# Attention and gated MLP on one core: the last two token chunks become one of 1024 tokens, worked in two stages

## The chip, the cores and the metric

The kernel runs on one core of a Trainium2 chip. The metric is the device time of one execution in microseconds (us). A profile of one execution gives the span of the program, the work of each engine and every instruction's start and length. PE is the matrix engine (PEld its weight loads), DVE the vector engine, ACT the scalar engine, POOL the GpSimd engine, SP the engine that issues most transfers; SPq and ACTq are transfers that SP and ACT issue.

## The reference

All inputs are fp32. The attention's queries are [8, 8, 576, 64] (batch, heads, tokens, features); keys and values are averaged over groups of 8 tokens, so each query sees 72 keys. The attention's output, as 4608 tokens of 512 features, goes through a layer of 2048 hidden features.

```
k_p, v_p = mean over 8 tokens of k, v            # 72 keys a head
attn     = softmax(q @ k_p.T / sqrt(64)) @ v_p
x   = attn.transpose(0, 2, 1, 3).reshape(4608, 512)
h   = x @ w_in                                   # 512 x 2048
g   = h * sigmoid(1.702 * h)
out = g @ w_out                                  # 2048 x 512
```

## The kernel before

**Precision.** Every product is made three times on rounded operands: each operand is split into a high part (a cast) and a low part (value minus cast), and high times high, low times high and high times low are added in the same bank of PSUM. A product of a block therefore is three matmuls for each 128 features that are summed over.

**Chunks.** Of each batch the first 512 tokens are a chunk (0 to 7); the last 64 tokens of the eight batches together are chunk 8. The tokens left over go through DRAM (left) until chunk 8 gathers them. Chunks 0 and 1 use plain products. Chunks 2 to 8 make h with seven products of blocks instead of eight: `pair(c, p)` (line 2345) takes pair p of eight (256 of the 2048 hidden features) and multiplies sums of blocks of the weights (tiles ws, 1.75 MB for a pair, fetched from DRAM by `fetch_pair` for every chunk anew) with sums of blocks of the tokens (x, xs, made by `combine`). Each of the seven products is six matmuls of 256 columns (line 2370) into the banks ha or hb. The helpers around them: `keep` (line 2385) copies a bank to SBUF, by ACT or DVE; `plus` (line 2392) adds a bank to the copy, on DVE; `gelu` applies the gate twice on ACT (lines 2409 and 2417), and line 2424 subtracts for the low part, on POOL or DVE.

**Output.** `outputs` (line 2556) gives blocks of 128 tokens by 512 output features, three matmuls of 512 columns each (lines 2572 to 2574), that are put between the products of the following pair and accumulate over the eight pairs in banks o. The weights w_out (tiles w1_0 to w1_15) stay in SBUF as high and low part. `finish` (line 2115) copies each o to SBUF and stores it; in chunk 8 by DVE or ACT (lines 2131 and 2143) with two stores of 128 KB for each copy.

**Order.** A planner in the program sorts all work by due times and costs into one list, two tables shift or swap single tasks of the list, and the list's order is that of each engine's queue.

## Time and profile before

| | before |
|---|---|
| time, median of 3 runs | 895.14 us (894.18 to 896.23) |
| span of the profiled execution | 893.6 us |
| PE busy | 880.5 us (99%) |
| DVE, ACT, POOL busy | 636.7 (71%), 543.8 (61%), 307.6 us (34%) |
| read from and written to DRAM | 150.47 and 25.17 MB |

The profiled execution has no time of its own beside its span: 893.6 us from the first to the last event of the program, 1.5 us less than the median of the runs. A busy share is an average over the program; idle time of an engine costs nothing unless something that sets the end waits for it. The three rounds of runs before spread over 2.05 us.

### The profile page before, as it was taken

To read this page: it belongs to the slowest core of one execution; us is meant where nothing else is said; L and a number is where in the kernel's file an instruction comes from. 1 tells how busy PE (TensorE), PEld (TensorE's weight loads), DVE (VectorE), ACT (ScalarE), POOL (GpSimd) and SP (SyncE) were. 2 spreads that over 40 slices of the span, in tenths; PEclk is the share of its full clock that TensorE was granted. 3 is DMA by queue.
4 is the path that set the end of the run, shared out by engine and by line. 5 is a ranking of instruction groups with operands and counts; after the bars stand their busy time and mean duration, and the time that the engine had idled before them with its cause. 6 is when DMAs were issued, how large, how long until landed. Compare 5 with 4: busy or idle time off the path is not lost.

```text
span 893.6 us, 15818 instructions
## 1 busy us (share of the span) xinstructions
PE 880.5 (99%) x5452; PEld 788.0 (88%) x5452; DVE 636.7 (71%) x1272; ACT 543.8 (61%) x1232; POOL 307.6 (34%) x301
## 2 busy tenths in 40 slices
PE   7999999999999999999999999999999999999997
...
PEclk9999999999999999999999999999999999999999
...
GB/s 262 378 242 65 195 71 197 201 171 189 170 273 166 229 229 250 225 176 218 229 230 155 231 187 263 165 205 231 218 192 154 199 232 184 172 187 212 165 143 47
DMA packets 145263, 176.68 MB, mean 198 GB/s; under 512 B 85664, under 2 KB 96928, under 8 KB 145184
## 3 DMA queue, kind: packets, MB, share of 16 engines
...
HBM read 150.47 MB, written 25.17 MB: 197 GB/s over the span
## 4 chain that ended last, share of the span: by engine, by line
PE 94%; SPq 2%; ACT 2%; DMA 1%; issue 0%; POOL 0%; DVE 0%; POOLq 0%; ACTq 0%
PE ha L2370 18%; PE hb L2370 14%; PE o L2574 12%; PE o L2573 12%; PE o L2572 12%; PE sps L1656 4%; PE h L2165 3%; PE h L2167 3%; PE h L2166 3%; PE o L2208 3%; PE o L2209 3%; PE o L2207 3%; PE pav L1895 1%; PE pav L1898 1%; PE pav L1897 1%; PE pav L1896 1%
## 5 line engine op out<-in xcount | busy, mean ns | idle before, releaser
L2574 PE MATMUL o<-w,glall 128*128 128x512 f32 x448 | 176.4, 394 | 0.0
L2572 PE MATMUL o<-w,ghall 128*128 128x512 f32 x448 | 176.3, 394 | 0.0
L2573 PE MATMUL o<-w,ghall 128*128 128x512 f32 x448 | 176.1, 393 | 0.0
L2424 POOL TENSOR_TENSOR glall<-shared,ghall 128x256 fp32r<-128x256 f32 x83 | 66.3, 804 | 215.5 <-ACT shared L2417 135.7
L2574 PEld LDWEIGHTS o<-w,glall 128*128 128x128 f32 x448 | 84.3, 188 | 18.5
L2409 ACT ACTIVATE ghall<-shared 128x256 fp32r<-128x256 f32 x150 | 61.3, 415 | 63.2 <-DVE shared L2392 32.5
L2370 PEld LDWEIGHTS ha<-xs,ws 128*128 128x128 f32 x672 | 93.1, 189 | 7.2 <-ACT shared L2385 0.8
L2370 PE MATMUL ha<-xs,ws 128*128 128x256 f32 x672 | 98.9, 283 | 0.0
L2370 PE MATMUL hb<-x,ws 128*128 128x256 f32 x672 | 94.5, 284 | 0.0
L2370 PEld LDWEIGHTS hb<-x,ws 128*128 128x128 f32 x672 | 88.8, 189 | 4.0 <-DVE shared L2392 0.3
L2572 PEld LDWEIGHTS o<-w,ghall 128*128 128x128 f32 x448 | 84.7, 189 | 8.5
L2573 PEld LDWEIGHTS o<-w,ghall 128*128 128x128 f32 x448 | 84.1, 188 | 8.6
L2392 DVE TENSOR_TENSOR shared<-shared,hb 128x256 f32<-128x256 f32 x112 | 46.6, 417 | 59.1 <-PE hb L2370 49.2
L2385 ACT COPY shared<-ha 128x256 f32<-128x256 f32 x93 | 34.4, 370 | 64.1 <-PE ha L2370 63.3
L2424 POOL TENSOR_TENSOR glall<-gall,ghall 128x256 fp32r<-128x256 f32 x46 | 35.6, 776 | 109.3 <-ACT gall L2417 75.5
L2165 PE MATMUL h<-x,w 128*128 128x256 f32 (+1 forms) x192 | 63.3, 329 | 1.5 <-ACT gh L2187 1.0
L2417 ACT ACTIVATE shared<-shared 128x256 f32<-128x256 f32 x150 | 60.8, 415 | 5.1 <-ACT osb L2125 1.3
L2167 PE MATMUL h<-x,w 128*128 128x256 f32 (+1 forms) x192 | 61.2, 319 | 0.0
L2166 PE MATMUL h<-x,w 128*128 128x256 f32 (+1 forms) x192 | 61.2, 319 | 0.0
L2424 DVE TENSOR_TENSOR glall<-shared,ghall 128x256 fp32r<-128x256 f32 x67 | 34.0, 509 | 38.1 <-ACT shared L2417 29.4
L2195 POOL TENSOR_TENSOR gl<-g,gh 128x512 fp32r<-128x512 f32 x28 | 39.5, 1410 | 48.9 <-ACT gh L2187 35.6
L1771 ACT COPY main<-sc 32x256 f32<-32x256 f32 (+2 forms) x109 | 48.7, 447 | 2.9 <-DVE sc L1728 1.1
(189 smaller groups left out, 2049.2 us busy)
## 6 DMA issues: line engine op xcount, KB each, us to landing
...
```

Of the source, the lines that this page charges most:

```text
L1771: copy(out=main()[32 * r : 32 * (r + 1), :, cols].rearrange("p j t (k a) -> p t j a k", a=2), in_=sc()[rows, ts, :, 16 * r : 16 * (r + 1)] ...
L2165: nc.tensor.matmul(o, lhsT=w[:, 0, j], rhs=xs[:, 0], start=j == 0, stop=False)
L2166: nc.tensor.matmul(o, lhsT=w[:, 1, j], rhs=xs[:, 0], start=False, stop=False)
L2167: nc.tensor.matmul(o, lhsT=w[:, 0, j], rhs=xs[:, 1], start=False, stop=j == NJ - 1)
L2370: nc.tensor.matmul(o, lhsT=wv()[:, r, jj], rhs=xo(k, jj), start=start and n == 0, stop=n == len(terms) - 1,  skip_group_check=not start,)
L2392: lambda: nc.vector.tensor_tensor(out=part(i), in0=part(i), in1=hb()[:, half * 256 : half * 256 + 256], op=ALU.add),
L2409: lambda: nc.scalar.activation(out=gh(), in_=src(), func=AF.Gelu_apprx_sigmoid),
L2417: lambda: nc.scalar.activation(out=part(i), in_=src(), func=AF.Gelu_apprx_sigmoid),
L2424: engine.tensor_tensor(out=gl(), in0=part(i), in1=gh().bitcast(F32), op=ALU.subtract)
L2572: nc.tensor.matmul(o(), lhsT=gh()[:, tok], rhs=w()[:, 0], start=start, stop=False)
L2573: nc.tensor.matmul(o(), lhsT=gh()[:, tok], rhs=w()[:, 1], start=False, stop=False)
L2574: nc.tensor.matmul(o(), lhsT=gl()[:, tok], rhs=w()[:, 0], start=False, stop=stop)
```

## The change

Chunks 7 and 8 are now one chunk (`LATE = 7`) of 1024 tokens, two halves of 512: batch 7's first 512 tokens and the 512 left tokens, all of which are gathered ahead of it (`gather_left`). Its operands (`late_op`, tiles y11, y21, y22, yt1 to yt4, each of 512 columns for two blocks) are made by `late_combine` and `late_split`; y22_1 takes the place of xs6_3, an operand that the last product hb6_7 of chunk 6 reads. The chunk runs in two stages, called stage B and stage C here.

Stage B, `hidden(p)` for all eight pairs in turn: seven products of six matmuls of 512 columns (new line 2154) into the banks la, lb and lc (a pair's lb takes the bank of the pair before); keep, plus and gelu are on 512 columns, and the gated h stays in SBUF (tiles store). Beside it `fold_out(p)` makes sums of the blocks of w_out on POOL and DVE and writes them to DRAM (768 KB for each pair).

Stage C, `outgoing(th, p)` for the two halves th of the tokens and the eight pairs: the sums of w_out come back (`fetch_sums`), `operands` makes sums and splits of the stored g (new lines 2325 and 2331), and seven products of six matmuls of 256 columns (new line 2376) accumulate over the eight pairs in seven banks m1 to m7. `combined(th)` then makes the four blocks of the output of seven banks, by one copy and seven additions on DVE (new line 2409), and stores 512 KB after each two blocks.

```diff
-    for c in range(FROM, B + 1):
+    for c in range(FROM, LATE):
...
+    def hidden(p):
...
+        product("11", "11", ha, True)
+        keep(at(0, 0), ha)
+        product("12", "21", hb, True)
+        plus(at(0, 0), hb)
+        gelu(at(0, 0))
+        product("s2", "t2", ha, False)
+        keep(at(0, 1), ha)
+        product("s1", "t1", hc, True)
+        product("s3", "t3", ha, False)
+        keep(at(1, 1), ha)
+        plus(at(1, 1), hc)
+        gelu(at(1, 1))
+        product("22", "t4", ha, False)
+        keep(at(1, 0), ha)
+        gelu(at(1, 0))
+        product("s4", "22", hc, False)
+        plus(at(0, 1), hc)
+        gelu(at(0, 1))
...
+    def late_combine(piece):
+
+        late_split("22", piece, "t2")
+        for out, a, b in (("t1", "t3", "t1"), ("t3", "t2", "t3"), ("t2", "t2", "t1"), ("t4", "t4", "t2")):
+            out, a, b = (x_whole(f"l{piece}", n) for n in (out, a, b))
+            less(out, a, b, a.refs() + b.refs(), out.refs())
+        for n in ("t1", "t3", "t2", "t4"):
+            late_split(n, piece, n)
...
+    def fold_out(p):
...
+            either(512, sums, [f], [(u, 2 * i), (u, 2 * i + 1)])
+        for out, a, b in ((0, 1, 0), (1, 3, 1), (3, 3, 0), (2, 3, 2)):
...
+            either(256, less_of, [(u, a), (u, b)], [(u, out)])
...
+    def operands(th, p):
...
+        parts_of(512, lambda: g()[:, :, 0:256], [g], a[0], a[1], ref(a[0]), ref(a[1]))
+        parts_of(256, at(1, 1), [g], lambda: a22()[:, 0], lambda: a22()[:, 1], (a22, 0), (a22, 1))
...
+        sums(views[1], at(1, 0), at(1, 1), ALU.add, [g], keys[1])
+        sums(views[3], at(0, 0), at(1, 0), ALU.subtract, [g], keys[3])
+        sums(views[2], views[1], at(0, 0), ALU.subtract, [g, keys[1]], keys[2])
+        sums(views[4], at(0, 1), views[2], ALU.subtract, [g, keys[2]], keys[4])
+        for s, u, names in ((s13, u13, (1, 3)), (s24, u24, (2, 4))):
+            parts_of(512, u, [keys[i] for i in names], s[0], s[1], ref(s[0]), ref(s[1]))
...
+    def outgoing(th, p):
...
+        a, t = operands(th, p), folded[p]
+        for m in "1675432" if p == NPAIR - 1 else "1245763":
...
+    def combined(th):
...
+        copy(512, lambda copy: copy(out=cells(a1), in_=bank("1")()), [bank("1")], [ref(a1)])
...
+        add(u2, a1, "6")
+        add(u3, u2, "7")
+        add(at(1, 1), u3, "5")
+        add(u2, u2, "5")
+        add(at(1, 0), u3, "4", ALU.subtract)
+        store_rows(th, 1, osbs[1])
+        add(at(0, 1), u2, "3")
+        add(at(0, 0), a1, "2")
+        store_rows(th, 0, osbs[0])
```

`either` and `sums` issue on POOL or, with the star below, on DVE; `parts_of` is a cast (ACT or DVE) and a subtraction by `either`. The planner and its tables are gone too: the order of all tasks is written out in a string `ORDER`, with a letter for the kind of work (P for PE, V for DVE, G for POOL, A for ACT, D for a transfer) and a star where a task goes to the other of its two engines, as in `*A:ah0_0#2 A:at0_0#0 A:at0_1#0`. PE's order is the same as before, row for row, up to the last matmul before chunk 7.

The first place is PE's start of chunk 7. Here ha7_0 and hb6_7 are banks of `pair`, o6 the output blocks of chunk 6, la, lb and lc the banks of `hidden`, and the x3 or x6 at a row's end counts matmuls. Before:

```order
L2370 MATMUL ha7_0_8582<-x7_8115,ws7_0_0_8372 128x256 x6
L2572 MATMUL o6_256_7700<-w1_12_1333,ghall1_2994 128x512
L2573 MATMUL o6_256_7700<-w1_12_1333,ghall1_2994 128x512
L2574 MATMUL o6_256_7700<-w1_12_1333,glall1_3077 128x512
L2572 MATMUL o6_384_7729<-w1_12_1333,ghall1_2994 128x512
L2573 MATMUL o6_384_7729<-w1_12_1333,ghall1_2994 128x512
L2574 MATMUL o6_384_7729<-w1_12_1333,glall1_3077 128x512
L2572 MATMUL o6_0_7629<-w1_14_1513,ghall0_2943 128x512
L2573 MATMUL o6_0_7629<-w1_14_1513,ghall0_2943 128x512
L2574 MATMUL o6_0_7629<-w1_14_1513,glall0_2961 128x512
L2370 MATMUL hb6_7_8502<-xs6_3_7411,ws6_7_2_8343 128x256 x6
```

Now, at the same place:

```order
L2154 MATMUL la0_8620<-y11_0_8144,ws7_0_0_8397 128x512 x3
L2154 MATMUL la0_8620<-y11_1_8166,ws7_0_0_8397 128x512 x3
L2086 MATMUL o6_256_7716<-w1_12_1349,ghall1_3010 128x512
L2087 MATMUL o6_256_7716<-w1_12_1349,ghall1_3010 128x512
L2088 MATMUL o6_256_7716<-w1_12_1349,glall1_3093 128x512
L2154 MATMUL lb0_8635<-y21_0_8187,ws7_0_0_8397 128x512 x3
L2154 MATMUL lb0_8635<-y21_1_8233,ws7_0_0_8397 128x512 x3
L2086 MATMUL o6_384_7746<-w1_12_1349,ghall1_3010 128x512
```

And 29 rows further, where the last output block of chunk 6 has been issued:

```order
L2154 MATMUL la0_8620<-yt2_0_8688,ws7_0_2_8509 128x512 x3
L2154 MATMUL la0_8620<-yt2_1_8690,ws7_0_2_8509 128x512 x3
L2154 MATMUL lb1_8753<-y21_0_8187,ws7_1_0_8546 128x512 x3
L2154 MATMUL lb1_8753<-y21_1_8233,ws7_1_0_8546 128x512 x3
```

Products of 512 columns in three banks stand where products of 256 columns stood; the output blocks of chunk 6 are between them as before, and after the last of those PE's queue holds products of `hidden` alone.

The second place is DVE's queue from the last product hb6_7 of chunk 6 on. L2392 before is `plus`; now L1904 is `plus` of `pair`, L1523 a low part of an operand, L1459 a sum of operands, L2221 a sum of w_out's blocks, L2171 `plus` of `hidden`. Before:

```order
L2392 TENSOR_TENSOR shared12_2909<-shared12_2909,hb6_7_8502 128x256
L2385 COPY gall_3045<-ha7_0_8582 128x256
L2392 TENSOR_TENSOR gall_3045<-gall_3045,hb7_0_8631 128x256
L2385 COPY shared12_2909<-ha7_0_8582 128x256
L2392 TENSOR_TENSOR shared12_2909<-shared12_2909,hb7_0_8631 128x256
L2424 TENSOR_TENSOR glall0_2961<-gall_3045,ghall0_2943 128x256
L2392 TENSOR_TENSOR gall_3045<-gall_3045,hb7_0_8631 128x256
```

Now, the rows from the fourth to the fifteenth row behind hb6_7's addition (the two rows of two inputs ahead of them are the low part of y22_1, 256 columns, and a sum of operands, 512 columns):

```order
L1516 CAST yt2_1_8690<-xtl1_1_7908 128x256
L1459 TENSOR_TENSOR xtl1_0_8452<-xtl1_0_8452,xtl1_1_7908 128x512
L1516 CAST yt2_1_8690<-xtl0_2_7958 128x256
L1523 TENSOR_TENSOR yt2_0_8688<-xtl1_1_7908,yt2_0_8688 128x256
L1523 TENSOR_TENSOR yt2_1_8690<-xtl0_2_7958,yt2_1_8690 128x256
L1523 TENSOR_TENSOR yt2_1_8690<-xtl1_1_7908,yt2_1_8690 128x256
L1516 CAST yt4_1_8707<-xtl0_0_8113 128x256
L1523 TENSOR_TENSOR yt4_0_8700<-xtl1_0_8452,yt4_0_8700 128x256
L1523 TENSOR_TENSOR yt4_1_8707<-xtl0_0_8113,yt4_1_8707 128x256
L1523 TENSOR_TENSOR yt4_1_8707<-xtl1_0_8452,yt4_1_8707 128x256
L2221 TENSOR_TENSOR u0_8730<-w1_1_483 128x512
L2171 TENSOR_TENSOR store0_0_8724<-store0_0_8724,lb0_8635 128x512
```

What DVE did for pair 0 of chunk 7 after hb6_7 (copies and additions of banks) has become the rest of the merged chunk's operands, and the addition that empties the bank lb0 stands behind all of them. POOL's queue holds, in the same stretch, five two-operand instructions of 256 columns (y22_1, yt2, the low part gl of pair 7 of chunk 6, yt4, one sum of u0) and three of 512 (two sums of operands and one of w_out's blocks).

The third place is the end of the program. PE before, the last two output blocks:

```order
L2572 MATMUL o8_384_9574<-w1_15_1577,ghall1_2994 128x512
L2573 MATMUL o8_384_9574<-w1_15_1577,ghall1_2994 128x512
L2574 MATMUL o8_384_9574<-w1_15_1577,glall1_3077 128x512
L2572 MATMUL o8_384_9574<-w1_14_1513,ghall1_2994 128x512
L2573 MATMUL o8_384_9574<-w1_14_1513,ghall1_2994 128x512
L2574 MATMUL o8_384_9574<-w1_14_1513,glall1_3077 128x512
```

PE now, the last pair of the second half, and DVE's last seven instructions (128x2x256 is the same 512 columns):

```order
L2376 MATMUL m1_1_9935<-w1_14_1529,oa1_7_10152 128x256 x6
L2376 MATMUL m6_1_9989<-shared11_9474,od1_7_10232 128x256 x6
L2376 MATMUL m7_1_9978<-ta7_9486,oc1_7_10210 128x256 x6
L2376 MATMUL m5_1_9967<-ta7_9486,oc1_7_10210 128x256 x6
L2376 MATMUL m4_1_9955<-w1_14_1529,ob1_7_10279 128x256 x6
L2376 MATMUL m3_1_9997<-w1_15_1593,od1_7_10232 128x256 x6
L2376 MATMUL m2_1_9944<-w1_15_1593,oa1_7_10152 128x256 x6
```

```order
L2409 TENSOR_TENSOR store0_1_8760<-store0_1_8760,m6_1_9989 128x512
L2409 TENSOR_TENSOR store1_1_8802<-store0_1_8760,m7_1_9978 128x512
L2409 TENSOR_TENSOR store0_1_8760<-store0_1_8760,m5_1_9967 128x512
L2409 TENSOR_TENSOR store3_1_9035<-store1_1_8802,m5_1_9967 128x2x256
L2409 TENSOR_TENSOR store3_1_9035<-store1_1_8802,m4_1_9955 128x2x256
L2409 TENSOR_TENSOR store2_1_8937<-store0_1_8760,m3_1_9997 128x2x256
L2409 TENSOR_TENSOR store2_1_8937<-store0_1_8760,m2_1_9944 128x2x256
```

Before, one copy follows the last matmul; now the last four products each are followed by an addition or two on DVE, in the order in which the banks end.

## Rows read from the trace of the kernel before

**Rows 1.** The page: the span, the engines' busy time (share of the span, instructions), and of the 40 equal slices of the span the busy tenths of PE and PE's granted clock in tenths of full speed.

```profile
span 893.6 us, 15818 instructions
...
PE 880.5 (99%) x5452; PEld 788.0 (88%) x5452; DVE 636.7 (71%) x1272; ACT 543.8 (61%) x1232; POOL 307.6 (34%) x301
...
PE   7999999999999999999999999999999999999997
...
PEclk9999999999999999999999999999999999999999
```

**Rows 2.** The page: the chain of work that ended last, shares of the span by engine.

```profile
PE 94%; SPq 2%; ACT 2%; DMA 1%; issue 0%; POOL 0%; DVE 0%; POOLq 0%; ACTq 0%
```

**Rows 3.** Timeline of PE around the start of chunk 7: start, length, what, how many. A row's length includes the depth of the matmul pipeline; the distance of two starts is what a matmul takes from the next.

```profile
711.79 0.39 PE L2573 MATMUL o<-w,ghall 128*128 128x512 f32 x1
712.02 0.39 PE L2574 MATMUL o<-w,glall 128*128 128x512 f32 x1
712.25 0.88 PE L2370 MATMUL ha<-x,ws 128*128 128x256 f32 x6
```

**Rows 4.** Windows: the stretch, its length, then busy us of PE, PEld, DVE, ACT and POOL (with counts), PE's granted clock, the busy share of the transfer engines, GB/s.

```profile
702.00:712.25 10.25, 10.25 (x66) 9.23 (x65) 9.34 (x15) 6.66 (x17) 7.96 (x6) 1.00 0.60 177
712.25:889.00 176.75, 176.71 (x1093) 158.45 (x1091) 57.17 (x135) 78.81 (x195) 18.13 (x16) 1.00 0.55 169
12.00:16.00 4.00, 2.29 (x20) 2.11 (x20) 2.47 (x5) 1.43 (x4) 1.04 (x1) 1.00 1.03 325
16.00:20.00 4.00, 2.47 (x18) 1.93 (x18) 3.48 (x8) 2.77 (x6) 1.04 (x1) 1.00 0.91 245
720.00:730.00 10.00, 10.00 (x65) 9.10 (x64) 3.79 (x6) 6.83 (x16) 9.92 (x8) 1.00 0.88 276
889.00:893.60 4.60, 0.00 (x0) 0.00 (x0) 0.00 (x0) 0.58 (x1) 0.00 (x0) 0.74 0.61 191
```

**Rows 5.** Timeline of PE in the last pair of chunk 8.

```profile
880.71 0.40 PE L2573 MATMUL o<-w,ghall 128*128 128x512 f32 x1
880.94 0.39 PE L2574 MATMUL o<-w,glall 128*128 128x512 f32 x1
881.17 0.88 PE L2370 MATMUL ha<-x,shared 128*128 128x256 f32 x6
881.88 0.39 PE L2572 MATMUL o<-w,ghall 128*128 128x512 f32 x1
```

**Rows 6.** Timeline of DVE, two-input instructions on SBUF (in brackets the idle time ahead).

```profile
704.38 1.26 DVE L2424 TENSOR_TENSOR glall<-gall,ghall 128x256 fp32r<-128x256 f32 x1
...
706.83 0.69 DVE L1973 TENSOR_TENSOR xt<-xt,xt 128x512 f32<-128x512 f32 x1 [0.22 <-POOL xt L1973]
...
721.57 0.74 DVE L2424 TENSOR_TENSOR glall<-gall,ghall 128x256 fp32r<-128x256 f32 x1 [1.17 <-ACT gall L2417]
...
727.59 1.36 DVE L2424 TENSOR_TENSOR glall<-shared,ghall 128x256 fp32r<-128x256 f32 x1
...
731.88 0.41 DVE L2424 TENSOR_TENSOR glall<-shared,ghall 128x256 fp32r<-128x256 f32 x1
```

**Rows 7.** Timeline of POOL in the same stretch.

```profile
704.07 1.30 POOL L1973 TENSOR_TENSOR x<-xt,x 128x512 fp32r<-128x512 f32 x1 [0.54 <-DVE x L1979]
...
707.59 0.74 POOL L2424 TENSOR_TENSOR glall<-gall,ghall 128x256 fp32r<-128x256 f32 x1 [0.79 <-PE ha L2370]
...
720.73 1.29 POOL L1973 TENSOR_TENSOR xt<-xt,xt 128x512 f32<-128x512 f32 x1
...
727.37 2.72 POOL L1973 TENSOR_TENSOR xs<-xt,xs 128x512 fp32r<-128x512 f32 x2
```

**Rows 8.** Groups of instructions by line and shape: busy us in all, mean ns of one, idle time ahead and its releasers.

```profile
L2424 POOL TENSOR_TENSOR glall<-shared,ghall 128x256 fp32r<-128x256 f32 x83 | 66.3, 804 | 215.5 <-ACT shared L2417 135.7 <-PE ha L2370 43.6 <-PE o L2574 12.6
...
L2392 DVE TENSOR_TENSOR shared<-shared,hb 128x256 f32<-128x256 f32 x112 | 46.6, 417 | 59.1 <-PE hb L2370 49.2 <-ACT shared L2385 8.7
...
L2195 POOL TENSOR_TENSOR gl<-g,gh 128x512 fp32r<-128x512 f32 x28 | 39.5, 1410 | 48.9 <-ACT gh L2187 35.6 <-DVE gh L2191 7.1 <-DVE sm L1722 5.5
...
L2182 ACT ACTIVATE g<-h 128x512 f32<-128x512 f32 x32 | 19.1, 598 | 25.2 <-PE h L2167 17.0 <-POOL gl L2195 6.9 <-DVE gl L2195 1.2
...
L1979 DVE CAST x<-xt 128x512 fp32r<-128x512 f32 x5 | 2.9, 573 | 0.0
...
L2098 DVE CAST w<-raw 128x512 fp32r<-128x512 f32 x6 | 2.4, 418 | 0.0
```

**Rows 9.** Timeline of the end.

```profile
887.62 0.69 DVE L2131 COPY osb<-o 128x512 f32<-128x512 f32 x1 [0.68 <-PE o L2574]
...
888.56 0.40 PE L2574 MATMUL o<-w,glall 128*128 128x512 f32 x1
889.00 0.58 ACT L2143 COPY osb<-o 128x512 f32<-128x512 f32 x1 [1.48 <-PE o L2574]
889.61 0.47 ACTq L2137 DMA_DIRECT2D out_dram<-osb  x1
889.77 0.55 SPq L2137 DMA_DIRECT2D out_dram<-osb  x1
```

**Rows 10.** Transfers from 884 to 894 us: GB/s in 40 slices of 0.25 us, and their sum.

```profile
GB/s 0 0 0 0 0 0 0 0 0 0 0 0 0 0 0 0 74 213 205 189 221 213 402 336 164 279 385 385 205 270 336 295 25 0 0 0 0 0 0 0
DMA packets 640, 1.05 MB, mean 105 GB/s; under 512 B 128, under 2 KB 128, under 8 KB 640
```

More of the change, by code (lines that the diff above doesn't have):

```diff
@@ L915, in swap @@
         self.other = mine
-def later(kind):
-    name = re.sub("^([^0-9]*)[3-9](?![0-9])", r"\1n", kind)
-    return name if name != kind else None
 class Plan:
@@ L1110, in order @@
+    def order(self):
+        named = {t.name: t for t in self.tasks}
+        placed, done = [], set()
+        for token in ORDER.split():
+            engine, name = token.lstrip("*").split(":")
+            t = named[f"{ENGINES[engine]} {name}"]
+            assert t.before <= done, t.name
+            if token[0] == "*":
+                t.swap()
+            placed.append(t)
+            done.add(t)
+        assert len(done) == len(self.tasks) == len(placed)
         return placed
@@ L1249, in attention_moe_kernel @@
     WHOLES = ("t1", "t4", "t3", "t2")
+    halves_of = [lambda t, k=k: t[:, k] for k in range(2)]
+    WHOLE_VIEWS = (halves_of * 2, halves_of + [lambda t: t] * 2)
     x_ops, x_wholes, shared = {}, {}, {}
@@ L1916, in weigh @@
                 parts_of, whole = (x[j],), None
+            elif b == LATE:
+                block, whole = late_op(("11", "21")[kh], jj), x_whole(f"l{piece}", ("t1", "t4")[kh])
+                parts_of = [block, whole.of]
             else:
@@ L1932, in weigh @@
                 hv, lv = (lambda j=j, r=r: x[j]()[:, r, cols] for r in range(2))
+            elif b == LATE:
+                hk, lk = ([(block, (r, piece))] for r in range(2))
+                hv, lv = (lambda block=block, r=r: block()[:, r, cols] for r in range(2))
             elif block:
@@ L1959, in weigh @@
                 )
+            elif npc > HALF:
+                ends = x_whole(f"l{piece}", ("t3", "t2")[kh])
+                copy(
+                    LEFT,
+                    lambda copy, jj=jj, pa=pa, ends=ends: copy(out=ends(jj)[:, HALF - LEFT :], in_=pa()[:, HALF:npc]),
+                    [pa],
+                    ends.refs((jj,)),
+                )
         if left is not None:
@@ L2001, in gather_left, with late_split, rest @@
             )
-        for n, src in (("11", "t1"), ("21", "t4"), ("22", "t2")):
-            split(x_op(c, n), x_whole(c, src))
-        combine(c)
+    def late_split(name, piece, source):
+        src = x_whole(f"l{piece}", source)
+        cols = slice(piece * HALF, (piece + 1) * HALF)
+        for jj in range(2):
+            y = late_op(name, jj)
+            copy(
+                HALF,
+                lambda copy, jj=jj, y=y: copy(out=y()[:, 0, cols], in_=src(jj)),
+                src.refs((jj,)),
+                [(y, (0, piece))],
+                sbuf=True,
+            )
+            def rest(engine, jj=jj, y=y):
+                engine.tensor_tensor(
+                    out=y()[:, 1, cols], in0=src(jj), in1=y()[:, 0, cols].bitcast(F32), op=ALU.subtract
+                )
+            pool(
+                HALF,
+                lambda rest=rest: rest(nc.gpsimd),
+                src.refs((jj,)) + [(y, (0, piece))],
+                [(y, (1, piece))],
+                other=lambda rest=rest: rest(nc.vector),
+            )
+    def late_combine(piece):
[5 more added lines that the diff above has]
+            late_split(n, piece, n)
     parts = [(f, m, 0, 512) for f in range(NF) for m in range(2)]
```

906 lines of the change are left out of this document (720 added, 186 removed), and 836 rows, old and new, of tables (PLACES, SWAPPED).

## The prediction

> **What bounds the kernel now.** I read the page first. PE is busy 880.5 of 893.6 us, every slice but the first and the last shows it full, and its granted clock, which is 2.4 GHz at full speed, shows a 9 (90% or more) in all 40 [rows 1]; the chain that ended last is PE for 94% [rows 2]. So the time is PE's column count as long as PE never waits. Then I looked where the change begins. PE's order is the same up to the matmul that starts at 712.25 us, the first product of chunk 7 [rows 3], and from there to 889.00 PE is busy 176.71 of 176.75 us, while DVE has 57.17, ACT 78.81 and POOL 18.13 us of work [rows 4]. Nothing waits there now; work that the other engines receive is free until they are late.
>
> **PE, counted.** The order has, from 712.25 on, 678 matmuls of 256 columns and 414 of 512 before, and 678 of 256 and 366 of 512 after: 42 x 8 of stage B and 30 that remain of chunk 6 are the 366, 42 x 16 of stage C and six of hb6_7 the 678. One of 512 takes 0.23 us from start to start (711.79, 712.02, 712.25 [rows 3]; 0.229 over the last pair, 880.71 to 881.17 [rows 5]), six of 256 take 0.71 to 0.72 (881.17 to 881.88). By these, 678 x 0.1195 + 414 x 0.229 = 175.8 us before, against 176.7 measured. After it is 48 x 0.229 = **11.0 us less**. Stage B is 8 x 9.6 = 77 us, stage C 16 x 5.02 = 80 us.
>
> **What the sums and operands cost.** A two-input instruction of DVE on SBUF takes 0.41 us for 256 columns when POOL rests (731.88) and 0.69 for 512 (706.83) [rows 6]. Beside POOL it is longer: one of 256 that starts at 721.57 ends at 722.31, while POOL runs from 720.73 to 722.02; one that starts at 727.59 inside a POOL instruction of 1.3 us takes 1.36; one at 704.38 takes 1.26, and POOL's ends at 705.37 [rows 6, 7]. Each time DVE ends 0.27 to 0.3 us after POOL's instruction, as if the two took turns and DVE did its last 0.27 (256 columns) behind it; for 512 I take 0.53. Of POOL's own, 256 columns take 0.74 and 512 take 1.29 to 1.30 [rows 7], so turns add up to 0.27 and 0.53 for DVE and 0.74 and 1.29 for POOL. Additions with a bank of PSUM do not show this: 417 ns on average over 112 [rows 8]. The Trainium skill, SBUF — State Buffer, section "SBUF: two separate sides", says the same as a rule: the port pair that DVE and GpSimd share is locked for a whole instruction, and the loser blocks. These rows agree (1.36 against 0.41 us); by DVE's undisturbed durations alone the first term below would be nothing.
>
> **Start of the merged chunk (stall A).** PE issues la0, two output blocks of chunk 6 and lb0, then another, and hb6_7's six matmuls end at 712.25 + 12 x 0.229 + 9 x 0.229 + 0.72 = 717.8. Then come lc0, a block, la1, five blocks and la0's second product: 717.8 + 6 x 0.229 x 3 + 18 x 0.229 = 726.0. There PE wants lb1, whose bank DVE empties by the addition of lb0 at the end of the piece of its queue that front shows. That queue starts when hb6_7 is read: a cast of y22_1 (its place held xs6_3), hb6_7's addition (0.42), some 718.8 us. Behind it are seven two-input instructions of 256 and three of 512, and POOL has five and three in the same stretch: 7 x 0.27 + 3 x 0.53 + 5 x 0.74 + 3 x 1.29 = 11.0 us if they take turns all the way. With lb0's addition of 0.7 the bank is free at 730.5, **4.5 us late**. PE's queue has all of pair 1 and the rest of pair 0 behind lb1, and so has ACT the gates; the lateness is met partly at earlier waits (operands yt2), but only once. If POOL and DVE do not collide, DVE alone ends at 718.8 + 7 x 0.41 + 3 x 0.69 + 4 casts of 0.4 + 0.7 = 726.1: nothing. If the four casts queue behind POOL too (573 ns beside 418 [rows 8] hints at it), it is 5.5 to 6. In the 10 us ahead, DVE has 9.34 and POOL 7.96 us of work already [rows 4], and the left tokens' operands, made for chunk 8 later before, now have to be made there, so I see no slack that would hide it. I take 4.5, bounds 0 and 6.
>
> **Stage B.** A pair has 9.6 us of PE. ACT has four gates of 0.6 [rows 8] and two or three copies of 0.58 [rows 9] and a cast or two: 5.1. POOL and DVE together have 16 sums of 512 columns, some thirty subtractions of 256 and the splits, over eight pairs: some 5 us of POOL and 2 us of DVE's share a pair. So none is full. But 13 of the 32 copies of the bank la, most of which the next product on the same bank waits for, are in DVE's queue, and one that stands behind a blocked instruction is ready 0.2 + 1.29 + 0.27 + 0.69 + 0.1 = 2.55 us after its product, where only one product of 1.37 us stands between: 1.2 us lost. I take one such meeting, **1.2**, bounds 0 and 4 (three or four). The transfers: 14 MB of weights in and 6 MB of sums out in 77 us are 260 GB/s, against 276 reached at a busy share of 0.88 [rows 4]. The first pairs' weights are issued while chunk 6 still runs, so I add nothing; late weights are in B's upper bound.
>
> **Stage C.** Lines 2325 and 2331 give DVE 56 instructions of 256 columns and 30 of 512, POOL 24 and 18. By turns that is 56 x 0.27 + 30 x 0.53 + 24 x 0.74 + 18 x 1.29 = 72.0 us, 4.5 a step of 5.02: it fits, and ACT's casts (three of some 0.6, one of 0.4, by its other work of these sizes) are 2.2 a step. At the border of the halves seven additions of 0.69 come on top (4.8 us) and the first step of the second half is only one step ahead. I take **0.6**, bounds 0 and 8.
>
> **The end.** Now one copy of 0.58 follows the last matmul, its two stores follow at 889.61 and 889.77, and the span ends 4.6 us after PE [rows 4, 9]. After, the last seven products end 0.72 apart and DVE's additions of 0.69 chain behind m6, with two for m5: the last ends 1.6 us after PE instead of 0.6. Two groups of stores of 512 KB close it in place of 256 KB; 1.05 MB took from 888 to 892.1 us, and near 300 GB/s in its second half [rows 10], so 256 KB more are 0.9. Together **+1.9**, bounds 1.0 and 2.5.
>
> **Sum.** -11.0 + 4.5 + 1.2 + 0.6 + 1.9 = -2.8 us. Against the profiled execution's span of 893.6 that is 890.8; the span is 1.5 below the median of the runs, and on the median's scale the forecast is **892.3 us**. Its own range, A from 3 to 6 and B and C between 1 and 4 together, is 889.5 to 895.4. A difference below 0.2% (1.8 us) cannot be told from none here.
>
> **Rivals.**
> *The lateness hardly occurs.* POOL's and DVE's instructions fall between each other, or POOL's gaps of waiting let DVE run. For it: from 720 to 730 us POOL was busy 9.92 us and DVE 3.79 [rows 4], and PE did not wait; the instruction at 731.88 took 0.41 between two of POOL's. Against it: in the start's piece both queues are full. Then -11.0 + 1.9 and at most 2 of stalls: 886 to 888. Chance 0.20.
> *Slower: stage C starves.* If the turns do not save DVE its first part and both pay full durations beside each other (0.42 and 0.69; 0.80 and 1.41 [rows 8]), the same 128 instructions are 56 x 0.42 + 30 x 0.69 + 24 x 0.80 + 18 x 1.41 = 88.8 us, and with 4.8 at the border 93.6, against 80.4 of PE and a lead of one step, 5.0: 8.2 us of waits. Then -11.0 + 4.5 + 1.2 + 8.2 + 1.9 = +4.8: 899.9. It is slower than before once C loses more than 3.4 us (0.21 a step), and by more than 0.2% from 5.2. For it: instructions of 1.26 and 1.36 as seen. Against it: the ends in [rows 6, 7] say 0.27. Chance 0.14, of which 0.02 within 0.2%.
> *The clock falls in a wait.* At 12 to 20 us PE was busy only 2.3 and 2.5 of 4 us and the granted clock stayed 1.00; after the last matmul, with PE at rest, it reads 0.74 over 4.6 us [rows 4]. If the 4.5 us of A are one pause and half the clock (1.2 GHz) holds for the next 5 us, 2.5 us are added, and every such pause in B or C adds as much: near 897 to 900. Chance 0.04. The Trainium skill, TensorE: Matmul & The Clock Gate, section "HAM oscillation — how this bites in real kernels", describes kernels whose pauses in a loop cost them the clock again and again; here the pauses I expect are split and the row at 12 us is against it.
> That the change does not do what it says is no case: 48 matmuls fewer stand in the order.
>
> **How the numbers follow.** The forecast has 0.62, of which 0.40 faster and 0.22 within 0.2% (above 893.4 when stalls pass 7.4 us). With the rivals: faster 0.60, same 0.24, slower 0.16. The range takes in the first rival's upper part and the second's lower: 886.5 to 897.5 leaves out about 0.07 below and 0.12 above.
>
> **What would show it.** PE's matmuls: 1044 from chunk 7 on at the same spacing (right). Waits of PE on DVE at la0's second operand or lb1, near 724 to 731 us, 4 to 5 us in sum; two-input instructions of DVE above 1 us beside POOL's. PE full in stage B but for 1 or 2 us, and in C for less than 1. Span's end about 6.5 us after the last matmul. It would be wrong if PE's idle time from 712 on sums to under 2 us or above 10, or if PE already waits ahead of 712 us, where the other engines' queues were rewritten too.

## The result and the profile after

The changed kernel is slower by 0.8%. Its median is 902.69 us over four runs (900.38 to 904.92) against 895.5 us before (894.18 to 896.23); the ratio is 1.0084 with a 95% interval of 1.0064 to 1.0104. The forecast was 892.3 us, and neither its range (886.5 to 897.5) nor its direction held.

The profiled execution has a span of 898.6 us where [rows 1] have 893.6; it is the fastest of the four (900.38 us, 2.3 below their median). From the page of the changed kernel, the span, the busy times and the chain, as in [rows 1, 2]:

```profile
span 898.6 us, 15882 instructions
...
PE 874.0 (97%) x5404; PEld 780.6 (87%) x5404; DVE 716.8 (80%) x1342; ACT 541.5 (60%) x1188; POOL 387.1 (43%) x377
...
PE 82%; DVE 4%; POOL 3%; issue 3%; ACT 3%; SPq 2%; DMA 2%; DVEq 0%; POOLq 0%; ACTq 0%
```

PE has 48 matmuls fewer (5404 in place of 5452) but is busy only 6.5 us less, where the count promised 11.0, and the chain that ended last is PE for only 82% where it was 94%: DVE, POOL and ACT are on it now.

Where the time went is seen by stretches. The windows of the changed kernel, with the columns of [rows 4], from the first product of chunk 7 (712.55) to PE's end (its last matmul ends at 892.0):

```profile
712.55:730.00 17.45, 13.32 (x60) 10.55 (x59) 12.59 (x19) 6.03 (x15) 8.72 (x8) 1.00 0.21 75
730.00:740.00 10.00, 10.00 (x38) 8.05 (x38) 4.01 (x8) 5.66 (x11) 1.47 (x2) 0.84 0.58 177
740.00:750.00 10.00, 7.21 (x26) 5.05 (x24) 5.29 (x9) 2.85 (x6) 6.74 (x7) 0.84 0.54 188
750.00:760.00 10.00, 9.33 (x39) 7.43 (x40) 8.19 (x14) 4.06 (x9) 8.02 (x7) 0.98 0.94 321
760.00:808.00 48.00, 46.19 (x200) 36.97 (x199) 34.89 (x55) 23.61 (x44) 27.22 (x26) 1.00 0.84 281
808.00:891.90 83.90, 83.90 (x687) 83.21 (x685) 71.24 (x100) 33.36 (x60) 42.81 (x37) 1.00 0.16 56
```

And a finer window behind the first pause, from the same view:

```profile
730.00:732.00 2.00, 2.00 (x6) 1.52 (x6) 0.58 (x2) 1.12 (x3) 1.26 (x2) 0.50 0.34 131
```

Ahead of stage C, PE has idle time and, from 730 to 760 us, a granted clock below 1, down to 0.50 (1.2 GHz) from 730 to 732; in stage C, from 808 us, it is full (83.90 of 83.90 us) at full clock. The timeline of PE has the waits themselves. Shown are the first product of chunk 7, every product or block that began behind a wait up to stage C (in brackets the idle time ahead of it and what ended it), the product ahead of the second pause, and PE's last product:

```profile
712.55 1.52 PE L2154 MATMUL la<-y,ws 128*128 128x512 f32 x6
...
724.80 0.50 PE L2088 MATMUL o<-w,glall 128*128 128x512 f32 x1 [0.70 <-POOL glall L1936]
...
729.43 2.61 PE L2154 MATMUL la<-yt,ws 128*128 128x512 f32 x6 [3.43 <-ACT store L2166]
...
742.73 1.52 PE L2154 MATMUL la<-y,ws 128*128 128x512 f32 x6
746.80 2.86 PE L2154 MATMUL lb<-y,ws 128*128 128x512 f32 x6 [2.54 <-DVE store L2171]
749.90 1.83 PE L2154 MATMUL la<-yt,shared 128*128 128x512 f32 x6 [0.24 <-ACT store L2166]
752.40 1.66 PE L2154 MATMUL lc<-y,ws 128*128 128x512 f32 x6 [0.67 <-DVE store L2171]
...
761.16 1.66 PE L2154 MATMUL la<-yt,shared 128*128 128x512 f32 x6 [0.31 <-DVE store L2166]
...
769.11 1.65 PE L2154 MATMUL la<-yt,ws 128*128 128x512 f32 x6 [0.85 <-DVE store L2166]
...
787.88 1.67 PE L2154 MATMUL la<-yt,ws 128*128 128x512 f32 x6 [0.65 <-ACT store L2166]
...
891.12 0.88 PE L2376 MATMUL m<-w,oa 128*128 128x256 f32 x6
```

From 712.55 to the end of the last product at 892.00 (891.12 + 0.88) it is 179.4 us, where the kernel before takes 176.7 (712.25 to 888.96). The count had promised 11.0 us less. So 13.7 us are lost in this stretch: 9.4 us are the waits above (4.1 in a first pause near 725 us, 3.45 in a second at 744 us and just behind it, 1.8 in three single waits), and the other 4.3 us are slow or restarting matmuls. The six matmuls behind the first pause take 2.61 us and those behind the second 2.86 instead of 1.52, and the windows from 730 to 760 sum to 3.4 us of clock not granted; a product behind a wait at full clock shows 1.66 in place of 1.52. Outside this stretch the start lies 0.3 us later and the end 6.6 us behind the last product instead of 4.6: 0.3 + 2.7 + 2.0 = 5.0 us, the difference of the spans. The medians lie 7.2 us apart; the other 2.2 us are in executions without a profile.

The first pause, by its queues. DVE's timeline (start, length, what, count):

```profile
721.64 1.77 DVE L1459 TENSOR_TENSOR xtl<-xtl,xtl 128x512 f32<-128x512 f32 x1
...
724.09 3.23 DVE L1523 TENSOR_TENSOR yt<-xtl,yt 128x256 fp32r<-128x256 f32 x3
...
727.24 0.81 DVE L1516 CAST yt<-xtl 128x256 fp32r<-128x256 f32 x1
727.97 1.08 DVE L1523 TENSOR_TENSOR yt<-xtl,yt 128x256 fp32r<-128x256 f32 x3
...
729.58 0.68 DVE L2171 TENSOR_TENSOR store<-store,lb 128x512 f32<-128x512 f32 x1
...
743.41 0.69 DVE L2221 TENSOR_TENSOR u<-w 128x512 f32<-128x512 f32 x1 [6.55 <-POOL w L2240]
```

POOL's and ACT's in the same stretch, one fence each:

```profile
719.76 3.11 POOL L1459 TENSOR_TENSOR xtl<-xtl,xtl 128x512 f32<-128x512 f32 x2 [0.42 <-DVE y L1523]
...
741.39 1.29 POOL L2240 TENSOR_TENSOR tf<-u,tf 128x512 fp32r<-128x512 f32 x1 [9.18 <-PE o L2087]
```

```profile
728.79 1.08 ACT L2166 COPY store<-la 128x512 f32<-128x512 f32 x2 [4.32 <-POOL u L2232]
```

DVE's addition of lb0 begins at 729.58 and ends at 730.26; the prediction had put that at 730.5. The casts and splits beside POOL take 0.8 to 1.1 us each (3.23 for three at 724.09), those behind POOL's last take 0.33 from one to the next (1.08 for three at 727.97). But PE resumed at 729.43 with la0's second product, and what it waited for was ACT's copy of la0, which began only at 728.79, 15 us after that bank was done. When lb1 came up, at 731.84, DVE's addition was over: lb1 did not wait.

The second pause is a chain through three queues. POOL had nothing to do for 9.18 us and began at 741.39, right behind the second matmul of the last output block of chunk 6 (it splits sums of w_out into a tile, tf, that takes the place of the tile ghall1, which this block reads). DVE's next sum of w_out began at 743.41, after 6.55 us of waiting for POOL. Behind it in DVE's queue stood the addition that empties lc0's bank, and for this bank PE waited from 744.26 to 746.80.

### The profile page after: what moved, and what is told of

It is laid out like the page before. It is cut to its first block, busy times and chain, and to the rows that moved or that the text cites. A ratio compares the mean times of both kernels' runs of the same rounds, so it can differ in the third digit from the quotient of the medians.

```text
span 898.6 us, 15882 instructions
## 1 busy us (share of the span) xinstructions
PE 874.0 (97%) x5404; PEld 780.6 (87%) x5404; DVE 716.8 (80%) x1342; ACT 541.5 (60%) x1188; POOL 387.1 (43%) x377
## 4 chain that ended last, share of the span: by engine, by line
PE 82%; DVE 4%; POOL 3%; issue 3%; ACT 3%; SPq 2%; DMA 2%; DVEq 0%; POOLq 0%; ACTq 0%
PE ha L1882 13%; PE hb L1882 10%; PE m L2376 9%; PE o L2086 8%; PE o L2087 8%; PE o L2088 8%; PE sps L1128 4%; PE h L1677 3%; PE h L1678 3%; PE h L1679 3%; PE o L1719 2%; PE o L1720 2%; PE o L1721 2%; PE la L2154 2%; POOL u L2221 1%
## 5 line engine op out<-in xcount | busy, mean ns | idle before, releaser
L2086 PE MATMUL o<-w,ghall 128*128 128x512 f32 x320 | 126.9, 397 | 0.0
L2087 PE MATMUL o<-w,ghall 128*128 128x512 f32 x320 | 126.1, 394 | 0.0
L2088 PE MATMUL o<-w,glall 128*128 128x512 f32 x320 | 125.0, 391 | 0.7 <-POOL glall L1936 0.7
L2088 PEld LDWEIGHTS o<-w,glall 128*128 128x128 f32 x320 | 60.1, 188 | 14.6 <-POOL glall L1936 1.1
L1882 PE MATMUL ha<-xs,ws 128*128 128x256 f32 x480 | 70.9, 283 | 0.0
L1882 PEld LDWEIGHTS ha<-xs,ws 128*128 128x128 f32 x480 | 66.0, 190 | 4.9 <-ACT shared L1897 0.8
L1882 PE MATMUL hb<-x,ws 128*128 128x256 f32 x480 | 67.2, 283 | 0.0
L2086 PEld LDWEIGHTS o<-w,ghall 128*128 128x128 f32 x320 | 60.6, 189 | 6.2
L1882 PEld LDWEIGHTS hb<-x,ws 128*128 128x128 f32 x480 | 63.4, 190 | 2.7 <-DVE shared L1904 0.2
L2087 PEld LDWEIGHTS o<-w,ghall 128*128 128x128 f32 x320 | 60.7, 190 | 5.6
L1904 DVE TENSOR_TENSOR shared<-shared,hb 128x256 f32<-128x256 f32 x81 | 33.5, 415 | 22.6 <-PE hb L1882 18.0
L1128 PE MATMUL sps<-k,qt 128*128 128x144 f32 x320 | 45.9, 287 | 1.7 <-ACT k L1035 0.7
L1128 PEld LDWEIGHTS sps<-k,qt 128*128 128x128 f32 x320 | 42.7, 190 | 4.1 <-ACT k L1035 1.1
```

What stands on the lines that cost most here:

```text
L1128: nc.tensor.matmul(ps()[:, t * PW : (t + 1) * PW], lhsT=qt()[:, s0 : s0 + P], rhs=m.k2()[:, jj], start=True, stop=True,)
L1882: nc.tensor.matmul(o, lhsT=wv()[:, r, jj], rhs=xo(k, jj), start=start and n == 0, stop=n == len(terms) - 1,  skip_group_check=not start,)
L2086: nc.tensor.matmul(o(), lhsT=gh()[:, tok], rhs=w()[:, 0], start=start, stop=False)
L2087: nc.tensor.matmul(o(), lhsT=gh()[:, tok], rhs=w()[:, 1], start=False, stop=False)
L2088: nc.tensor.matmul(o(), lhsT=gl()[:, tok], rhs=w()[:, 0], start=False, stop=stop)
```

## The experiments

All edits are of the string that sets the order, unless said; lines of only "..." stand for what is left out. The median of before was 895.06 us beside e1, e2, e4 and e5, and 894.77 beside e9, e6 and e7; the ratios are to these. The changed kernel's 902.69 us was not measured again with either set.

**e1: the pauses filled.** Two repeats of a product whose bank nobody reads yet are put in each pause.

```diff
+REPEATS = {'PE o6_128#15': ('PE lc7_0#0', 2), 'PE la7_2#0': ('PE lc7_1#0', 2)}
...
             t.emit()
+            what, times = REPEATS.get(t.name, ("", 0))
+            for _ in range(times):
+                named[what].emit()
```

> The changed kernel with PE's two longest pauses at the start of the merged chunk (725.2 to 729.4 us, and 744.2 to 746.8 us) filled by repeating a product whose operands and bank are ready: lc0's six matmuls twice more ahead of la0's second product, and lc1's twice more ahead of lb2. The waits themselves stay. Theory that the clock is a cost of its own: in the changed kernel's trace the granted clock is 0.50 to 0.72 for some 3 us behind each pause, about 3.4 us in sum; filled, it stays at 1.00 from 712 to 760 us, the span falls by 3 us or more from 898.6 and the median from 902.7 to about 896 to 898, since the other executions of the changed kernel had a still lower mean clock (0.988 to 0.990). Rival, that the slow stretch is not from the pauses: clock and time stay as they are, 900 to 903 us or up to 1 us above for the repeated matmuls.

Measured: 899.61 us (899.43 to 900.33), ratio to before 1.0056 (1.0041 to 1.0071). The windows of e1 from 730 to 750 us:

```profile
730.00:740.00 10.00, 9.27 (x42) 7.43 (x40) 5.97 (x11) 6.86 (x13) 1.48 (x2) 1.00 0.53 178
740.00:750.00 10.00, 8.54 (x38) 6.56 (x36) 5.29 (x9) 2.81 (x6) 6.75 (x7) 1.00 0.54 185
```

The clock is 1.00 where the changed kernel has 0.84 twice. From the first product of chunk 7 (714.09) to PE's end (891.95) it is 177.9 us in place of 179.4, although 24 matmuls were added. The profiled span itself is 898.5 us, the same as the changed kernel's, since this execution's chunk 7 starts 1.5 us later. The expected fall of the span by 3 us and of the median to 896 to 898 was too large: a part of the slow stretch had lain over waits that follow (la's wait behind the second pause is 1.46 us now, 0.24 before). Still the median is 3.1 us lower by doing more work, and the executions agree within 0.9 us where the changed kernel's spread over 4.5; its three other executions had a mean clock of 0.988 to 0.990 and spans of 900.7 to 903.1 us against 0.995 and 898.6 in the profiled one. So the clock is a cost of its own, 1.6 us between the profiled stretches and about 3 in the median.

**e2: the last output block of chunk 6 earlier.**

```diff
-P:o6_128#15 A:osb6_256#0 V:store0_0#0 P:la7_0#1
+P:o6_128#15 A:osb6_256#0 V:store0_0#0 P:o6_384#15 P:la7_0#1
...
-A:store0_1#3 P:o6_384#15 *A:tf1_2#0
+A:store0_1#3 *A:tf1_2#0
```

> One edit of the order: the last output block of chunk 6 (o6_384 of its last feature block, three matmuls) is issued ahead of la0's second product instead of some 15 us later. Theory for the second pause: POOL's split of the first sums of w_out takes a tile that this block still reads, DVE's sum for pair 1 stands behind POOL's, and the addition that empties lc0's bank for lb2 stands behind it on DVE; so the pause at 744.2 us (2.5 us, with 0.24 and 0.67 behind it and some 1.5 us of clock) goes, and 0.7 us of the first pause is filled: 4 to 5.5 us less than the changed kernel's 902.7, 897 to 899 us. Rival, that the second pause is the first one's lateness passed on or late weights: it stays, and the time is within 1 us of 902.

Measured: 898.07 us, ratio 1.0034 (1.0020 to 1.0047). PE's timeline of e2, the products behind waits up to 760 us, and its window from 740:

```profile
725.71 0.50 PE L2081 MATMUL o<-w,glall 128*128 128x512 f32 x1 [0.69 <-POOL glall L1929]
...
730.35 2.93 PE L2147 MATMUL la<-yt,ws 128*128 128x512 f32 x6 [2.76 <-ACT store L2159]
...
746.40 1.65 PE L2147 MATMUL la<-yt,shared 128*128 128x512 f32 x6 [0.76 <-ACT store L2159]
...
753.21 1.65 PE L2147 MATMUL la<-yt,ws 128*128 128x512 f32 x6 [1.08 <-ACT store L2159]
```

```profile
740.00:750.00 10.00, 9.24 (x41) 7.31 (x41) 6.85 (x11) 4.18 (x9) 6.74 (x7) 1.00 1.00 361
```

The wait of 2.54 us for lc0's bank is gone, and with it the clock's second fall (1.00 from 740 to 750); the first pause is 0.7 us shorter (3.45 us). Shorter waits for copies of la have come in its place (0.76 and 1.08), so that all waits from 712 us on fall from 9.4 to 7.1 us. The second pause was this block's place in the order, not the first one's lateness.

**e4: hb6_7 earlier.**

```diff
-A:gh6_7#1 P:la7_0#0 A:cs6_7#5
+A:gh6_7#1 P:la7_0#0 P:hb6_7#2 A:cs6_7#5
...
-P:o6_0#14 P:hb6_7#2 D:ws7_1#2
+P:o6_0#14 D:ws7_1#2
```

> One edit of the order: the last product hb6_7 of chunk 6 is issued right behind la0 instead of 3.4 us later, so that the place of its operand is free for y22_1 earlier and DVE's and POOL's queue of splits begins 3.3 us earlier. Theory: this queue sets the first pause, so that pause shrinks from 4.1 us to 1 us or less, and the clock holds there: 4 to 5 us less than the changed kernel's 902.7, 898 to 899 us, while the second pause stays. Rival, that the first pause is set by something else that ACT's copy waits for (the memory of the earlier tiles, or weights): the pause ends at the same time and the time is within 1 us of 902.

Measured: 895.4 us (894.32 to 899.06 in ten runs), ratio 1.0003 (0.9986 to 1.0019): the change's whole loss against before, by one place in the order. PE's timeline of e4 up to 750 us, and its window from 740:

```profile
728.05 1.64 PE L2147 MATMUL lb<-y,ws 128*128 128x512 f32 x6 [0.30 <-DVE store L2164]
...
742.42 1.66 PE L2147 MATMUL lb<-y,ws 128*128 128x512 f32 x6 [2.54 <-DVE store L2164]
745.50 1.66 PE L2147 MATMUL la<-yt,shared 128*128 128x512 f32 x6 [1.41 <-ACT store L2159]
748.03 1.65 PE L2147 MATMUL lc<-y,ws 128*128 128x512 f32 x6 [0.87 <-DVE store L2164]
```

```profile
740.00:750.00 10.00, 5.30 (x21) 3.72 (x22) 8.63 (x15) 4.49 (x9) 7.23 (x8) 1.00 0.88 279
```

The first pause has shrunk to 0.30 us. The second stays with 2.54, 1.41 and 0.87 us, and there the clock does not fall (1.00 from 740 to 750). The median fell by 7.3 us where 4 to 5 were expected. In the profile the stretch from la0 to the last product (713.70 to 887.87) is 5.3 us shorter than the changed kernel's, and of that the waits are only 2.1 (7.3 in sum, 9.4 before); the larger part is the 3.4 us of clock, both falls of which are gone.

**e5: POOL's work of the start given to DVE.** Seven of POOL's instructions become DVE's, at the same places.

```diff
-G:y2_1#1
+*G:y2_1#1
...
-G:xtl0_2#0
+*G:xtl0_2#0
...
-G:xtl0_0#1
+*G:xtl0_0#1
...
-G:yt2_0#0
+*G:yt2_0#0
...
-G:gl6_7#3
+*G:gl6_7#3
...
-G:yt4_0#0
+*G:yt4_0#0
...
-G:u1_0#0
+*G:u1_0#0
```

> Seven of POOL's two-input instructions in the stretch from 718 to 728 us (four of 256 columns, three of 512) are given to DVE at the same places of the order; the work is the same. Theory of turns (DVE and POOL exclude each other): DVE alone needs twelve of 0.33 from start to start, six of 0.61 and the casts, some 9 us in place of 11.4, so the first pause ends 2 to 2.5 us earlier, near 727 us: 2 to 4 us less than the changed kernel. Rival, that DVE's long instructions there are only slow and POOL works beside it: DVE's queue gets 3.5 us longer, the pause ends near 733 us, and the time is 3 to 5 us above the changed kernel's 902.7.

Measured: 896.87 us (895.42 to 897.65 in ten runs), ratio 1.0025 (1.0015 to 1.0034). DVE's timeline of e5, some of its two-input instructions of the start, and PE's row behind the first pause (chunk 7 starts at 714.05 in this execution):

```profile
720.93 1.29 DVE L1453 TENSOR_TENSOR xtl<-xtl,xtl 128x512 f32<-128x512 f32 x2
...
723.95 1.42 DVE L1517 TENSOR_TENSOR yt<-xtl,yt 128x256 fp32r<-128x256 f32 x4
...
728.37 0.68 DVE L2165 TENSOR_TENSOR store<-store,lb 128x512 f32<-128x512 f32 x1
```

```profile
727.71 1.67 PE L2148 MATMUL la<-yt,ws 128*128 128x512 f32 x6 [0.76 <-ACT store L2160]
```

With seven instructions more, DVE is through with lb0's addition 15.0 us behind the start of chunk 7 (728.37 + 0.68 - 714.05); with POOL's help it took 17.7 (730.26 - 712.55). Two of 512 columns take 1.29, four of 256 take 1.42. So the work of DVE and POOL had held each other up, as the theory of turns says, and the rival's longer queue is out. The pause is 0.76 us. The median fell by 5.8 us where 2 to 4 were expected; here too the clock is 1.00 from 730 to 750 us.

**e9: la0's copy into memory of its own.** In the code, pair 0's first copy and lb0's addition go to a tile that no earlier stage holds; the gate writes the stored h.

```diff
+        own = buf(moe, [P, 2, 256], F32, "g", "tz0_0", bufs=1) if p == 0 else None
+        first = Part(own, 0, lambda t: t.rearrange("p a d -> p (a d)")) if p == 0 else at(0, 0)
...
-        keep(at(0, 0), ha)
+        keep(first, ha)
         product("12", "21", hb, True)
-        plus(at(0, 0), hb)
-        gelu(at(0, 0))
+        plus(first, hb)
+        gelu(at(0, 0), first if p == 0 else None)
```

> The changed kernel where only the first copy of pair 0 (bank la0) and lb0's addition go to a tile of their own in place of the stored h's tile, which lies in the memory of the attention's tiles; the gate then writes the stored h. Theory that la0's copy waits for the attention's memory (for the last reads of the operands' sums), not for the bank: la0's second product starts when its operands are there, 2 to 4 us earlier than the 729.4 us of the changed kernel (17 us behind its first product), and the rest of the pause, up to 730.3 us, moves to lb1, which waits for DVE's queue as predicted; with a shorter half-speed stretch the time falls 1 to 2.5 us, 900 to 901.5. Rival, that ACT's queue or the operands hold the copy anyway: no change, within 1 us of 902.

Measured: 901.07 us (900.24 to 901.75), ratio 1.0067 (1.0054 to 1.0080). That is in the expected range and also within 1 us of 902, where the rival had it, and the changed kernel's four runs reach from 900.38 to 904.92: the time decides nothing, the rows do. ACT's copy of la0 and the next copy, PE's timeline, and the window behind the pause, of e9:

```profile
724.42 0.58 ACT L2162 COPY tz<-la 128x512 f32<-128x512 f32 x1
728.96 0.59 ACT L2162 COPY store<-la 128x512 f32<-128x512 f32 x1 [3.96 <-POOL u L2228]
```

```profile
725.89 1.30 PE L2147 MATMUL la<-yt,ws 128*128 128x512 f32 x5
727.45 0.50 PE L2147 MATMUL la<-yt,ws 128*128 128x512 f32 x1 [0.27 <-DVE yt L1516]
730.40 2.93 PE L2147 MATMUL lb<-y,ws 128*128 128x512 f32 x6 [2.44 <-DVE tz L2167]
```

```profile
730.00:740.00 10.00, 9.60 (x30) 7.76 (x31) 4.17 (x8) 4.71 (x10) 1.52 (x2) 0.68 0.55 184
```

The copy of la0 begins at 724.42 instead of 728.79, while the next copy, into a tile of the stored h, still begins at 728.96. la0's second product begins 13.3 us behind the first instead of 16.9, waits 0.27 for its last operand, and then lb1 waits 2.44 us, until 730.40. So the copy of la0 had waited for its place, in the memory of earlier tiles, and not for ACT's queue or the bank (which of the earlier tiles held it is not shown); and the wait for lb1 that the prediction named is there once this one is gone, at the time it named.

**e6: e2 and e4 together.** Both edits of the order, nothing else.

> The two edits of the order together: hb6_7 right behind la0, and the last output block of chunk 6 ahead of la0's second product. Theory that the two pauses at the start of the merged chunk have separate causes and add up: each edit alone took 4 to 7 us from the changed kernel's 902.7 (898.1 and 895.4); together both pauses and the slow clock behind them are gone, 890.5 to 892.5 us, below the kernel before. Rival, that with one pause gone the other is only moved (weights or DVE's and POOL's work are the bound): 894 to 896 us.

Measured: 892.43 us (890.77 to 894.31), ratio 0.9973 (0.9961 to 0.9985), 0.3% faster than before. All of PE's waits above 0.2 us from 712 us on (sum, count, longest):

```profile
PE la L2147 <- ACT store L2159: 3.3, 3, 1.5
PE la L2147 <- DVE store L2159: 0.9, 1, 0.9
```

Both pauses are gone and four waits of 0.7 to 1.5 us for copies of la are left. The two causes were separate: the median fell by 10.3 us, where e2's 4.6 and e4's 7.3 add up to 11.9. In the profile the stretch from la0 to the last product (712.43 to 883.23) is 8.6 us shorter than the changed kernel's: 5.2 of waits (4.2 in sum, 9.4 before) and 3.4 of clock.

**e7: e6, and both ends of the change.** Two moves ahead of chunk 7, the last two pairs bank by bank, and the last 512 KB stored in two halves. The diff leaves out e6's two moves.

```diff
-P:pav7_0#2 A:yt1_0#0 G:gl6_3#3 *A:cs6_4#3 P:o6_128#7
+A:yt1_0#0 G:gl6_3#3 *A:cs6_4#3 P:o6_128#7 P:pav7_0#2
...
-V:mt7_1#3 P:ha6_7#0 *A:ah7_1#3 A:xtl1_0#1 V:al7_1#3 A:xtl1_1#1 A:y1_1#2 V:y1_0#2
+V:mt7_1#3 V:y1_0#2 P:ha6_7#0 *A:ah7_1#3 A:xtl1_0#1 V:al7_1#3 A:xtl1_1#1 A:y1_1#2
...
+P:m1_1#6 P:m1_1#7 P:m6_1#6 P:m6_1#7 A:store0_1#4 P:m7_1#6 P:m7_1#7 V:store0_1#2 P:m5_1#6 P:m5_1#7 V:store1_1#2
+P:m4_1#6 P:m4_1#7 V:store0_1#3 V:store3_1#2 P:m3_1#6 P:m3_1#7 V:store3_1#3 O:store3_1#0 P:m2_1#6 P:m2_1#7
+V:store2_1#2 O:store2_1#0 V:store2_1#3 O:store2_1#1
...
         add(at(0, 1), u2, "3")
+        if th:
+            store_rows(th, 0, osbs[0], 1)
         add(at(0, 0), a1, "2")
-        store_rows(th, 0, osbs[0])
+        store_rows(th, 0, osbs[0], 0 if th else None)
```

> e6's edits and two more. Ahead of chunk 7: the product pav7_0_2 is issued one output block later and the low part of y11's third piece one place earlier on DVE, against the two waits of PE on DVE at 675 and 701 us (0.69 and 0.43 us in the changed kernel's trace). At the end: the last two pairs of the second half are taken bank by bank, so that the banks are done 1.4 us apart in place of 0.7 us and DVE's additions keep up, and the last 512 KB are stored in two halves. Theory: 1.1 us less ahead of chunk 7, and the end falls from 6.7 us behind the last matmul to 4.9, so 2.5 to 3 us less than e6: 888 to 889.5 us. Rival, that the operands of the last pair are not ready earlier on DVE: PE waits in stage C and 1 us at most is won at the end, 890 to 891 us.

Measured: 889.96 us (889.06 to 892.86 in six runs), ratio 0.9950 (0.9937 to 0.9963): 4.8 us below before, the best of both kernels and all edits. It is 2.5 us less than e6, at the lower edge of what was expected; the time itself lies 0.5 us above the expected 888 to 889.5. Its page's first line, and DVE's last addition:

```profile
span 887.8 us, 15885 instructions
```

```profile
883.17 0.69 DVE L2402 TENSOR_TENSOR store<-store,m 128x512 f32<-128x512 f32 x1 [0.75 <-PE m L2369]
```

The last addition ends at 883.86, 0.7 us behind the last product (883.13), and the span 4.7 us behind it, where the changed kernel needs 6.6: 1.9 us of e7's gain. The two waits ahead of chunk 7 are gone but for 0.24 us. No run has one of these edits alone.

## Why the prediction was wrong

**PE's count held.** 48 matmuls of 512 columns fewer at the same spacing (0.227 us, 712.55 to 713.91 for six). Stage C, with two products of stage B between its own, takes 83.5 us (808.47 to 892.00), all busy: 80.8 without those two, where the count had 80.

**Stall A was right in size, in part by luck.** Predicted 4.5 us, measured 4.1, but the wait was another: 0.70 us for a low part from POOL and 3.43 for la0's copy. lb1, for which the prediction had it, did not wait. What the prediction did not see is that la0's copy needs memory of earlier tiles and stands ahead of lb1; e9 shows both waits. The size agrees because both end with the same queues of DVE and POOL. DVE's queue ended 17.7 us behind the start of chunk 7 (730.26), against 18.25 by turns of DVE and POOL (730.5 for a start at 712.25), and by e5 DVE alone is through 2.7 us sooner. The Trainium skill, SBUF — State Buffer, section "SBUF: two separate sides", says that of a DVE instruction with two SBUF inputs and a GpSimd instruction that reads SBUF the one that starts first has the shared pair of ports for all its length, and the other is blocked. e5's rows agree (15.0 against 17.7 us). The sum of turns had no casts; casts of 256 columns, 0.4 us in the line without collisions, took 0.8 beside POOL and 0.28 without it.

**Stage B is a step that failed.** The term was 1.2 us with bounds 0 and 4; the waits there sum to 5.3 (3.45 and 1.8). The mechanism that I priced, copies behind blocked instructions in DVE's queue, is of the kind and size of two of the three single waits (0.31 and 0.85 us; the third, 0.65, is for a copy by ACT). The 3.45 us are another: a tile for the sums of w_out whose place the last output block of chunk 6 still reads, and two queues behind it. I had named DVE's place for these sums only as work that takes a port, not what POOL's split waits for. The order would have shown it, and I read past it: the text on the first place says that the last output block of chunk 6 has been issued where PE's queue goes on with la0's second product, but one more, o6_384 on w1_14, stands seven products of `hidden` later. e2 took the pause away by moving it.

**The clock is the other: a rival with 0.04 and nothing in the sum, and it came.** I had argued from the row at 12 to 20 us that the clock would hold. It fell behind both pauses, for 3.4 us by the windows; with restarts it is 4.3 us of the profiled execution, as much as stage B's excess of 4.1, and e1 puts the price of the falls at 1.6 us net in the profiled stretch and 3.1 in the median. It is what carried the time out of the range: with the measured waits and end but no clock the sum is -11.0 + 0.3 + 9.4 + 2.0 = +0.7, some 896 on the median's scale and inside. The rival's price, 5 us at half clock behind a pause, was too high for one pause here: 3.4 us of loss by the windows are 6.8 us at half clock, for two pauses. The Trainium skill, TensorE: Matmul & The Clock Gate, section "HAM oscillation — how this bites in real kernels", describes a matmul kernel that loses the clock anew at each wait of its loop. The rows here agree in kind, with two pauses that no loop repeats. The row that I argued from was one execution: in e5's profile the clock did fall there, from some 19 to 22 us. It reads 0.94 from 10 to 20 us and 0.89 in the next window, where the kernel before has 1.00:

```profile
20.00:30.00 10.00, 9.46 (x60) 8.09 (x60) 8.46 (x20) 7.14 (x16) 5.51 (x5) 0.89 0.96 332
```

The changed kernel's longer executions are those with the lower mean clock (spans of 898.6 us at 0.995 to 903.1 at 0.988). In e4's ten runs it is not so: the fastest has 0.994, where most have 0.997 or 0.998.

**Ahead of 712 us I had nothing in the sum.** Waits there were one of the prediction's signs of being wrong, without a price. The chunk's operands are made earlier by DVE, and PE waits for it twice where it did not before:

```profile
675.11 0.38 PE L1367 MATMUL pav<-ah,vh 128*128 128x256 f32 x1 [0.69 <-DVE y L1418]
...
701.32 0.38 PE L1367 MATMUL pav<-ah,vh 128*128 128x320 f32 x1 [0.43 <-DVE y L1418]
```

These 1.1 us are in all the variants but e7. In the profiled execution of the changed kernel PE was busy for 24.4 of the first 30 us, against 23.5 before, so that its chunk 7 starts only 0.3 us late; in e1 to e5 it starts at 713.5 to 714.1.

**Stage C and the end.** C: predicted 0.6, measured 0; the slower rival, that stage C starves, is out. The 72 us of turns fit. The end: predicted +1.9, measured +2.0.

By parts: -11.0 + 0.3 + 4.1 + 5.3 + 4.3 (clock and restarts) + 0 + 2.0 = +5.0 us between the profiled spans, against the forecast's -2.8. (The forecast's own range, by its bounds, is 890.0 to 896.0 and not 889.5 to 895.4.)

**What stays open.** Why the clock fell behind some pauses and not behind others. It fell behind 3.45 us of waits near 725 us in e2 (0.69 and 2.76; 0.83 from 730 to 740 us) and behind 3.4 us in e9 (0.70, 0.27 and 2.44; 0.68), but not behind 2.54, 1.41 and 0.87 us at 740 to 748 in e4 and much the same in e5 and e9, though the changed kernel lost it at that place behind 2.54 us. At the start of the program it held before and fell in e5, with PE busier ahead of it (4.0 of 6 us at 12 to 18 us, against 3.4 before). No run here tells apart what decides it.
